# Pacing bulk loads, four tap buffers and grouped TensorE switches in a planned convolution and feed-forward kernel

## Chip, cores and metric

The kernel runs on one core of one Trainium2 chip. The metric is the device time of one execution in microseconds (us). A measurement of this kernel is the median of several executions.

## What is computed

The reference mixes a state-space convolution and a feed-forward layer by a gate that depends on the token. Cut to what matters (2048 tokens, 640 channels, 128 states, 1728 hidden columns, all float32):

```python
g = sigmoid((u * gate_w).sum(-1, keepdims=True))           # one gate per token
K = 2 * einsum("dn,dnl->dl", C, exp(A*dt * arange(2048))).real  # 2048 filter taps for each of 640 channels
y = irfft(rfft(u.T, 4096) * rfft(K, 4096))[:, :2048].T     # causal convolution along the tokens
a = y + u * D_skip
b = relu(u @ w1) @ w2                                      # 640 -> 1728 -> 640
out = g * a + (1 - g) * b
```

## The kernel before

**The feed-forward part.** Each float32 matrix is split into a high and a low half, and a product is three TensorE matmuls (high x high, high x low, low x high). The 1728 hidden columns are worked in three passes (`PARTS`, five, five and four slices of 128). A pass goes over 8 groups of 256 tokens. In the first pass `trans` turns the tokens (tile `xx`) and stores the halves in DRAM (`xt`), `hidden` makes hidden values from them, and `sums` multiplies by w2 and stores partial sums (`part`). In passes two and three `wide` makes hidden values for a pair of groups (matmuls of 512 columns, written W below), `sums` makes four sums a group (matmuls of 320 columns, S below), and `reload` brings the halves of the next pair back from `xt`: 1280 KB a group, two DMAs, both issued by one planned task.

**The convolution part.** First the taps are generated: phases, exponentials, sines and short matmuls (tiles `sn`, `cs`, `mg`, `G`, `pk`) give the taps, which go to DRAM as `kd`. Generation runs beside the first two passes. Then `conv` transforms in five groups of 128 channels, beside the rest of the feed-forward work. For a group: `load_k` brings four parts of the taps (`ck`, two buffers), `load_u` the tokens (`xu`, one buffer, 1 MB in two DMAs); `stage1` is four tasks for taps (K) and four for tokens (U), each of 8 recorded matmuls into a PSUM buffer `pc`, emptied by two VectorE transposes into the tile `ku`, which holds the K half and the U half of a group. `stage2` is eight tasks of 32 recorded matmuls; ScalarE copies one result into K's block, VectorE makes two products, one of them into `kx` (three buffers, `KX`), and GpSimd adds. `inv2` is two steps of 128 short matmuls; `relay` is eight VectorE transposes from U back into K; `inv1` is four tasks of two matmuls (Y below), whose results ScalarE scales by the gate into `yo` (two buffers, `YO`). From `yo` they go to the output, after GpSimd has added the feed-forward sum (`yj`), or to DRAM (`y_`), to be added in the last pass. PSUM has three `pc` buffers, shared by all these steps.

**What sets the order.** Every step is a task of the class `Plan` with an engine, a queue, a cost set by hand, its dependencies, and the buffers (rings) that it takes and uses. `Plan.run` goes through planned time: for each engine it takes the head of a queue with the lowest priority number among those that are ready, and adds half a rank to a task whose mode differs from the engine's current one (`f` for the feed-forward and for phases and exponentials, `t` for taps, `c` and `c1` for the convolution). For TensorE it also looks `HOLD` = 0.3 ahead: a task of better priority that is nearly ready is waited for. It has a cost for loading TensorE's code, once in 128 matmuls, greater when a bulk transfer is under way. A chosen task's instructions are emitted at once, and `Pinned` (line 287 in the profile, for all of them) keeps them in that order. So the order on every engine, and on SyncE (SP), which issues nearly all DMAs one after another, is fixed when the program is built. An instruction that has to wait holds up all that stand behind it on its engine.

Of the kernel before, what the change touches and what calls it, by code (L numbers as in the profile page):

```python
# [31 lines left out]
KX = 3  # L32
# [22 lines left out]
S2D = 1  # L55
# [6 lines left out]
YO = 2  # L62
YJ = 2
# [79 lines left out]
class Plan:  # L143
# [7 lines left out]
    SLACK = .8  # L151

# [53 lines left out]

    def run(self):
        self.free = {e: 0.0 for e in self.LAG}
        mode, dma, log, done, block = {}, 0.0, [], 50.0, 0.0
        heads = {k: 0 for k in self.queues}  # L210
        while True:
            best = None
            for e in self.LAG:
                c, soon = [], []
                for (eng, q), n in heads.items():
                    if eng == e and n < len(self.queues[eng, q]):
                        t = self.queues[eng, q][n]
                        r, known = self.ready(t)
                        for g in t.glue:
                            r2, k2 = self.ready(g)  # L220
                            r, known = max(r, r2), known and k2
                            for b in t.take:
                                k = sum(x.ring is b.ring for x in (*t.take, *g.take))
                                r = max(r, sorted(b.ring.slots)[k - 1] if len(b.ring.slots) >= k else 1e9)
                        (c if known else soon).append((r, t))
                if not c:
                    continue
                at = max(self.free[e], min(r for r, _ in c))
                key = lambda t: t.prio + (0.5 if t.mode is not None and mode.get(e) not in (None, t.mode) else 0)
                r, t = min((x for x in c if x[0] <= at), key=lambda x: key(x[1]))  # L230
                start = max(at, r)
                if e == 'PE':

                    for r2, t2 in c:
                        if key(t2) < key(t) and r2 <= at + self.HOLD:
                            t, start = t2, max(at, r2)
                    hold = [r2 for r2, t2 in soon if t2.prio < t.prio and r2 <= at + self.HOLD]
                    if hold:
                        at = max(hold)
                if best is None or at < best[0]:  # L240
                    best = at, e, t, start
            if best is None:
                break
            _, e, t, start = best
            change = self.CHANGE.get(e, 0) if t.mode is not None and mode.get(e) not in (None, t.mode) else 0
            if t.mode is not None:
                mode[e] = t.mode
            for b in t.take:
                b.ring.slots.remove(min(b.ring.slots))
            t.fn()  # L250
            self.free[e] = start + change + t.dur
            if e == 'PE':

                done += t.n
                while done >= 128:
                    done -= 128
                    at = self.free[e] - t.dur * done / t.n
                    fetch = self.FETCH + (self.BUSY if dma > at + 2 else 0)
                    self.free[e] += max(0, block + fetch - at)
                    block = max(at, block + fetch)  # L260
            if t.port:

                self.free[e] += 0.25 * min(max(self.free['POOL'] - start, 0), t.dur)
            t.end = self.free[e] + t.lag
            if t.kb:
                dma = max(dma, start + min(t.dur, 0.62) + 0.5) + t.kb / (230 if start < 12 else 270)
                t.end = max(dma, start + t.dur) + 1.1
            for b in (*t.take, *t.use):
                b.left -= 1
                b.free = max(b.free, t.end)  # L270
                if b.left == 0:
                    b.ring.slots.append(b.free)
            heads[e, t.q] += 1
            log.append((start, t))
# [6 lines left out]
class Pinned:  # L281
# [3 lines left out]
    def __getattr__(self, name):  # L285
        f = getattr(self._eng, name)
        return lambda *a, **k: self._tc.keep_in_program_order(f(*a, **k))  # L287
# [21 lines left out]
class Kernel:  # L309
    def __init__(self, tc, ctx, io, out):  # L310
# [4 lines left out]
        self.plan, self.late_loads = Plan(), []  # L315
# [23 lines left out]
    def feed_forward(self):  # L339
# [151 lines left out]
        def reload(p, g):  # L491
            x_ = xtok[p, g] = tok('xhl')

            def load():
                for l in range(2):
                    D_.dma_start(self.xx[:, l, g % 2].bitcast(F32), sc['xt'][g][l])
            X[p, g] = [A('SP', 'x', 1.25, load, [xst[g], xst[7]], take=[x_], kb=1280, rank=2)]

        W, H, done, stq = {}, {}, {}, S if STQ == 'ACT' else D_
# [111 lines left out]
        def sums(p, g, j, q_, qld):  # L611
# [16 lines left out]
            def pe(ks):  # L628
                def go():
                    if ks[0] == 0:  # L630
                        st['sb', g, j] = pb.tile([128, 320], F32, name="pf")
                    for k in ks:
# [3 lines left out]
                                      start=k == 0, stop=k == np_ - 1)  # L636
                return go
# [14 lines left out]
            for k in range(0, np_, 4 if j == 0 else 5):  # L652
# [4 lines left out]
                           use=[w for _, w in ws] + list(ht) + ([b_] if k else []), mode='f'))  # L657
            e = A('ACT' if p == 0 else 'DVE', 'ff', 0.38 if p == 0 else 0.43, out, a + qld, take=[q_] if p == 0 and j == 0 else (),
# [88 lines left out]
        for p, n in enumerate(PARTS):  # L747
# [3 lines left out]
            for k, g in enumerate(order):  # L751
# [28 lines left out]
                if not last:  # L780
# [5 lines left out]
                    continue  # L786
                to, ds = CG[g] * 128, []
                for t in range(2):
# [16 lines left out]
                    es = [sums(p, g, j, q_, mx[t]) for j in (2 * t, 2 * t + 1)]  # L805
                    if CG[g] == 5 and g <= FIRST:
                        es.append(with_last(g, t, q_, es))
# [355 lines left out]
    def conv(self, C=128):  # L1163
# [5 lines left out]
        for k, v in dict(psc=3, ck=2, cu=1, kx=KX, yo=2, yj=2, K=2).items():  # L1169
            ring(k, v)  # L1170
# [16 lines left out]
        def load_k(i, q):  # L1187
            k_ = tok('ck')

            def go():  # L1190
                t = st['ck', i, q] = self.early.tile([128, 16, 32], F32, name="ck", bufs=2)
# [6 lines left out]
        def load_u(i):  # L1198
            u_ = tok('cu')

            def go():
                if i == 0:
                    self.xu = self.early.tile([128, 4 * D], F32, name="xu")
                t = st['cu', i] = self.xu[:, :16 * C].rearrange("p (b d) -> p b d", d=C)
                for h in range(2):
                    D_.dma_start(t[64 * h:64 * h + 64], ud[:, 16 * h:16 * h + 16, i * C:i * C + C])
            return u_, A('SP', 'cu', 1.6, go, [], take=[u_], kb=1200, rank=2.5 if i else 6)
# [9 lines left out]
        def paired(x, order):  # L1217
            return x.rearrange(f"p (j e m t) -> {order}", j=8, m=4, t=2)


        def stage1(kind, i, q, src):
# [15 lines left out]
            def turn(h):  # L1237
                def go():
                    if k and q == 0 and h == 0:
                        st['ku', i] = self.pr.tile([128, 2, 32 * C], F32, name="ku", bufs=2)  # L1240
                        st['K', i], st['U', i] = st['ku', i][:, 0], st['ku', i][:, 1]
# [9 lines left out]
            a = A('PE', 's' + kind, 0.87, pe, [ld, tf, opened] + ([] if k else [first[i]]), take=[b_, buf] if new else [b_], use=[s_] if new else [s_, buf],  # L1251
# [12 lines left out]
        def stage2(i, j, dep):  # L1264
            b_, x_ = tok('psc'), tok('kx')

            def pe():
                ps = self.psc.tile([128, 2, 4, C], F32, name="pc")
                for a in range(2):
                    for m in range(4):  # L1270
                        for p in range(2):
                            r, g = slice(p * 64, p * 64 + 64), 4 * j + m
                            x = st['ku', i].rearrange("p k (j e m t) -> p j m k e t", j=8, m=4, t=2)
                            self.E.matmul(ps[32 * m:32 * m + 32, p, 2 * a:2 * a + 2].rearrange("q k (e t) -> q k e t", t=2),
                                          st['tm'][r, g, 32 * a:32 * a + 32], x[r, j, m], start=True, stop=True)
                st['p2', i, j] = ps.rearrange("q p (a k) c -> q k a p c", a=2)

# [3 lines left out]
            def mul(a):  # L1281
                def go():
                    k = whole(i, j)
                    if a:
                        st['kx', i, j] = self.pr.tile([128, 2, 2, C], F32, name="kx", bufs=KX)
                    V.tensor_mul(st['kx', i, j] if a else k, st['p2', i, j][:, 1, None, a].to_broadcast([128, 2, 2, C]), k)
                return go

            def add(k):
                def go():  # L1290
                    y, x = whole(i, j)[:, k], st['kx', i, j][:, 1 - k]
# [4 lines left out]
            for a in (1, 0):  # L1296
                c.append(A('DVE', 's2', 0.62, mul(a), c, take=[x_] if a else (), use=[b_, K[i]] + [x_] * (1 - a), rank=S2D))
            return f, [A('POOL', 's2', 0.7, add(k), c, use=[x_, K[i]], rank=1) for k in range(2)]


        def whole(i, j):
            return st['K', i][:, 512 * j:512 * j + 512].rearrange("q (b p c) -> q b p c", b=2, p=2)


        def inv2(i, h, dep):
# [14 lines left out]
            def back(k):  # L1320
                def go():
                    S.copy(st['U', i].rearrange("q (h g m c) -> q h m g c", h=2, m=4, c=C)[:, h, 2 * k:2 * k + 2],
# [11 lines left out]
        def relay(i, r, dep):  # L1334
            d = slice(r * 16, r * 16 + 16)
            return A('DVE', 'rl', 0.95, lambda: V.transpose(out=st['K', i].rearrange("p (j d m) -> p d j m", j=8, m=4)[:, d],
                                                            in_=st['U', i].rearrange("p (j m d) -> p d j m", j=8, m=4)[:, d]),
# [5 lines left out]
        def inv1(i, j, dep):  # L1343
            last = i == n - 1
            for q in range(2):
# [8 lines left out]
                def pe(q=q, b0=b0):  # L1354
                    py = st['p4', i, b0] = self.psc.tile([128, 2, 4, C], F32, name="pc")
                    for h in range(2):
                        x = (h * 16 + b0) * C
                        self.E.matmul(py[h * 64:h * 64 + 64, 0].rearrange("p b c -> p (b c)"), st['tw'],
                                      st['K', i][:, x:x + 4 * C], start=True, stop=True)

                def copy(q=q, b0=b0, ns=ns, y_=y_, first=first):
                    if first:
                        self.gy = self.pr.tile([128, 2, 32 * C], F32, name="ku", bufs=2)[:, 0].rearrange("p (b c) -> p b c", c=C)
# [55 lines left out]
        self.u_first = u[1]  # L1419
# [4 lines left out]
        for i in range(n):  # L1424
            more = i + 1 < n
            if more:
                u = load_u(i + 1)
            fs = [stage2(i, j, [*dep, tm]) for j in range(8)]
# [61 lines left out]
```

## Time and profile before

| What | Value |
|---|---|
| Median of 3 runs | 666.48 us (666.0 to 666.77) |
| The profiled execution's own time | 668.51 us |
| Its span, first to last instruction | 666.7 us |
| VectorE busy | 524.2 us (79%), 818 instructions |
| ScalarE busy | 402.0 us (60%), 603 instructions |
| GpSimd busy | 93.7 us (14%), 133 instructions |
| Main DMA queue | 76058 packets, 101.16 MB, 50.8% of 16 engines |

The page gives the busy time of every engine, the span in 40 slices, and the chain of work that ended last. The first 60% of the span is the feed-forward passes one and two beside the generation of taps; from about 410 us on, the convolution runs beside pass three. "Issue" is a wait that no recorded event explains. A busy TensorE counts from the first matmul's start to the modelled end of the last, so short pauses between matmuls do not all show as idle.

### The profile page before, as it was taken

The page shows a single profiled execution, that of the slowest core. Times are in us where ns is not written, and L with a number is a line of the kernel's source. Part 1 is how long each engine was busy: PE and PEld are TensorE (multiplying, and loading weights), DVE is VectorE, ACT ScalarE, POOL GpSimd, SP SyncE. Part 2 cuts the span into 40 slices and gives each one's busy share as a digit, 9 for nine tenths or more (in the row PEclk, how much of TensorE's full clock was granted, in tenths as well). Part 3 has the DMA queues.
Part 4 walks back from the last instruction along what each step waited for, and adds up shares of the span by engine and source line. Part 5 has one row for each costly group of instructions (what it writes and reads, how often), then busy time and mean ns, then how long its engine had stood idle before and what let it go on. Part 6 is the DMA issues. An engine that isn't in the chain of part 4 may idle for free.

```text
span 666.7 us, 19238 instructions
## 1 busy us (share of the span) xinstructions
PE 630.3 (95%) x8236; PEld 505.5 (76%) x8236; DVE 524.2 (79%) x818; ACT 402.0 (60%) x603; POOL 93.7 (14%) x133
## 2 busy tenths in 40 slices
PE   7989999999999999999999999998999897978997
PEld 7989999899887887888998986845666444733666
DVE  5799838989999998989999985584995375977462
ACT  5467449998999989889789922042430541353431
POOL 0000000000000000000000000060600260623632
PEclk9999999999999999999999999999999997989999
DMA  9965744323364642441543149954068639245256
GB/s 264 315 214 184 238 143 159 113 73 135 105 198 123 235 121 65 174 151 57 199 144 96 57 146 286 293 169 97 3 218 177 191 96 249 62 120 132 59 167 137
DMA packets 76303, 102.80 MB, mean 154 GB/s; under 512 B 7609, under 2 KB 59449, under 8 KB 75962
## 3 DMA queue, kind: packets, MB, share of 16 engines
q1 hardware_dynamic: 76058, 101.16, 50.8%
q8 instruction: 65, 1.06, 0.7%
q10 hardware_dynamic: 160, 0.41, 0.2%
q14 instruction: 20, 0.16, 0.1%
HBM read 62.36 MB, written 39.19 MB: 152 GB/s over the span
## 4 chain that ended last, share of the span: by engine, by line
PE 60%; DVE 17%; DMA 9%; issue 4%; SPq 4%; ACT 3%; POOL 1%; DVEq 0%; ACTq 0%; POOLq 0%
PE pf L287 37%; PE pc L287 12%; PE pk L287 5%; SPq L287 4%; DMA xu<-in_A_u_dram 3%; DVE G L287 3%; DVE sn L287 3%; PE pg L287 2%; PE px L287 2%; DVE ku L287 2%; DMA ck<-kd 2%; DVE mg L287 2%; DVE cs L287 1%; DVE kx L287 1%; PE pe L287 1%
## 5 line engine op out<-in xcount | busy, mean ns | idle before, releaser
L287 PE MATMUL pf<-xx,w1h 128*128 128x256 f32 (+1 forms) x760 | 184.8, 340 | 2.1 <-issue 1.4
L287 PEld LDWEIGHTS pf<-xx,w1h 128*128 128x128 f32 x760 | 124.8, 189 | 27.9 <-issue 13.1
L287 PE MATMUL pf<-xx,w1l 128*128 128x512 f32 (+1 forms) x340 | 115.7, 340 | 0.0
L287 ACT COPY ku<-pc 128x512 f32<-128x512 f32 (+1 forms) x60 | 42.8, 731 | 91.7 <-PE pc L287 91.4
L287 PE MATMUL pf<-w2h,hh 128*128 128x320 f32 x288 | 90.4, 318 | 2.4 <-DVE hl L287 1.3
L287 PE MATMUL pf<-w2l,hh 128*128 128x320 f32 x288 | 88.0, 310 | 0.0
L287 PE MATMUL pf<-w2h,hl 128*128 128x320 f32 x256 | 74.1, 315 | 0.3 <-issue 0.3
L287 DVE STREAM_TRANSPOSE ku<-pc 128x512 f32<-128x512 f32 x80 | 50.8, 687 | 24.8 <-PE pc L287 24.7
L287 PEld LDWEIGHTS pf<-xx,w1l 128*128 128x128 f32 x340 | 64.3, 189 | 7.7 <-DVE w1l L287 0.2
L287 POOL TENSOR_TENSOR ku<-ku,kx 128x256 f32<-128x256 f32 x80 | 56.5, 739 | 96.2 <-DVE ku L287 38.6
L287 POOL TENSOR_TENSOR kt<-kt,dsk 128x8 f32<-128x8 f32 x20 | 10.1, 504 | 389.5 <-DVE kt L287 363.4
L287 PEld LDWEIGHTS pf<-w2h,hh 128*128 128x128 f32 x288 | 54.3, 189 | 10.8 <-issue 6.1
L287 PEld LDWEIGHTS pf<-w2l,hh 128*128 128x128 f32 x288 | 54.4, 189 | 0.5
L287 ACT ACT_TABLE_LOAD x42 | 53.9, 1283 | 0.7
L287 DVE TENSOR_TENSOR sn<-pg,cs 128x1024 f32<-128x1024 f32 x40 | 48.6, 1215 | 5.9 <-ACT cs L287 5.7
L287 DVE STREAM_TRANSPOSE ku<-ku 128x512 f32<-128x512 f32 x40 | 40.7, 1077 | 15.5 <-ACT ku L287 15.4
L287 ACT CAST cs<-pg 128x1024 int32<-128x1024 f32 x40 | 40.4, 1010 | 20.6 <-PE pg L287 20.5
L287 PEld LDWEIGHTS pf<-w2h,hl 128*128 128x128 f32 x256 | 46.7, 189 | 6.7 <-issue 6.3
L287 DVE TENSOR_TENSOR mg<-mg,cs 128x1024 f32<-128x1024 f32 x40 | 48.9, 1222 | 1.6
L287 ACT ACTIVATE cs<-cs,half_pi 128x1024 f32<-128x1024 f32 x40 | 45.6, 1141 | 0.0
L287 PE MATMUL pc<-ku,tm 64*32 64x256 f32 x1280 | 43.2, 397 | 0.5 <-DVE ku L287 0.5
L287 ACT ACTIVATE sn<-sn 128x1024 f32<-128x1024 f32 x40 | 42.2, 1055 | 0.2
(169 smaller groups left out, 1249.1 us busy)
## 6 DMA issues: line engine op xcount, KB each, us to landing
xx<-xt SPq DMA_DIRECT2D x24, 640.0 KB, 6.8
xt<-xx SPq DMA_DIRECT2D x16, 640.0 KB, 3.7
part<-q SPq DMA_DIRECT2D x16, 640.0 KB, 3.5
q<-part SPq DMA_DIRECT2D x16, 640.0 KB, 4.6
ws<-in_B_w_dram SPq DMA_DIRECT2D x20, 320.0 KB, 4.8
kd<-kt SPq DMA_DIRECT2D x80, 64.0 KB, 1.9
ck<-kd SPq DMA_DIRECT2D x40, 128.0 KB, 4.1
xu<-in_A_u_dram SPq DMA_DIRECT2D x10, 512.0 KB, 11.4
```

Source lines behind the costliest of these rows:

```text
L287: return lambda *a, **k: self._tc.keep_in_program_order(f(*a, **k))
```

## The change

Six edits that go together:

1. **Planner.** While TensorE is in mode `f`, a convolution task is taken only if `burst` finds at least `GATHER` = 2 tasks of modes `c` or `c1` that could run in a row, or if `PATIENCE` = 3 have passed since the last task that was not `f`; otherwise the best ready `f` task is taken. The 0.3 look-ahead no longer applies between two `f` tasks.
2. **Reload of xx.** One task of two DMAs becomes two tasks of one DMA (640 KB). In pass three, three of the four tasks of a pair wait for the last matmul of a named sum (`last_of`, `mark`, `behind`); the wait stands on SyncE.
3. **Load of xu.** For groups 2 to 4 (counted from 0) the two DMAs become eight (128 KB each), two behind each of the first four `stage2` tasks of the group before.
4. **Taps.** Parts 1 and 3 of groups 1 to 4 (counted from 0) have two buffers of their own (`cl`), so there are four.
5. **Products over U's block.** `ku` is laid out so that the K and U parts of a block of 512 lie next to each other; the product that went to `kx` goes over U's part of the block, and `kx` is gone.
6. **Buffers of yo.** Three in place of two. The planned cost of a relay step goes from 0.95 to 1.02.

```diff
-KX = 3
...
-YO = 2
+YO = 3
...
+    BURST, GATHER, PATIENCE = ('c', 'c1'), 2, 3
...
+    def burst(self, c, heads, at):
+        run, end, taken = 0, at, {}
+        for _, t in sorted((x for x in c if x[1].mode in self.BURST), key=lambda x: x[0]):
+            for x in self.queues['PE', t.q][heads['PE', t.q]:][:self.GATHER]:
+                if x.mode not in self.BURST or any(d.end is None or d.end > end + .1 for d in x.deps):
+                    break
+                fits = True
+                for b in x.take:
+                    k = taken[b.ring] = taken.get(b.ring, 0) + 1
+                    fits = fits and k <= len(b.ring.slots) and sorted(b.ring.slots)[k - 1] <= end + .1
+                if not fits:
+                    break
+                run, end = run + 1, end + x.dur
+        return run
...
-                if e == 'PE':
+                if e == 'PE' and mode.get(e) == 'f':
+
+
+                    if t.mode in self.BURST and at - since < self.PATIENCE and self.burst(c, heads, at) < self.GATHER:
+                        other = [x for x in c if x[1].mode == 'f' and x[0] <= at + .05]
+                        if other:
+                            r, t = min(other, key=lambda x: key(x[1]))
+                            start = max(at, r)
+                if e == 'PE' and (t.mode != 'f' or mode.get(e) != 'f'):
...
+            if e == 'PE' and t.mode != 'f':
+                since = start + t.dur
...
+    def behind(self, ins, mark):
+        info = mybir.DependencyInfo(mybir.DependencyClass.Sync, mybir.DependencyReason.DATA)
+        self._tc.add_manual_dep(ins.ins, mark, info, reason="paced")
...
-            def load():
-                for l in range(2):
-                    D_.dma_start(self.xx[:, l, g % 2].bitcast(F32), sc['xt'][g][l])
-            X[p, g] = [A('SP', 'x', 1.25, load, [xst[g], xst[7]], take=[x_], kb=1280, rank=2)]
-
+            def load(l):
+                x = D_.dma_start(self.xx[:, l, g % 2].bitcast(F32), sc['xt'][g][l])
+                for t in X[p, g][l].deps:
+                    if t in self.mark:
+                        D_.behind(x, self.mark[t])
+            X[p, g] = [A('SP', 'x', 0.62, lambda l=l: load(l), [xst[g], xst[7]], take=() if l else [x_], use=[x_] if l else (),
+                         kb=640, rank=2) for l in range(2)]
...
+                if k % 2 == 0 and k < 6:
+                    paced = [x for i in order[k + 2:k + 4] for x in X[p, i]]
...
+                    for x in (paced[1:3], paced[3:])[t] if k % 2 == 0 and k < 6 else ():
+                        x.deps += (last_of[p, g, 2 * t + (x is not paced[1])],)
...
-            k_ = tok('ck')
+            own = q % 2 and i
+            k_ = tok('ckp' if own else 'ck')
...
-            def go():
-                if i == 0:
-                    self.xu = self.early.tile([128, 4 * D], F32, name="xu")
-                t = st['cu', i] = self.xu[:, :16 * C].rearrange("p (b d) -> p b d", d=C)
+            def go(k):
+                if k == 0:
+                    if i == 0:
+                        self.xu = self.early.tile([128, 4 * D], F32, name="xu")
+                    st['cu', i] = self.xu[:, :16 * C].rearrange("p (b d) -> p b d", d=C)
+                t, b = st['cu', i], slice(k * 16 // n, (k + 1) * 16 // n)
                 for h in range(2):
-                    D_.dma_start(t[64 * h:64 * h + 64], ud[:, 16 * h:16 * h + 16, i * C:i * C + C])
-            return u_, A('SP', 'cu', 1.6, go, [], take=[u_], kb=1200, rank=2.5 if i else 6)
+                    x = D_.dma_start(t[64 * h:64 * h + 64, b], ud[:, 16 * h:16 * h + 16, i * C:i * C + C][:, b])
+                    if behind:
+                        D_.behind(x, self.mark[behind[k]])
...
-                        st['ku', i] = self.pr.tile([128, 2, 32 * C], F32, name="ku", bufs=2)
-                        st['K', i], st['U', i] = st['ku', i][:, 0], st['ku', i][:, 1]
+                        st['ku', i] = self.pr.tile([128, 8, 2, 512], F32, name="ku", bufs=2)
+                        st['K', i], st['U', i] = st['ku', i][:, :, 0], st['ku', i][:, :, 1]
...
-                    if a:
-                        st['kx', i, j] = self.pr.tile([128, 2, 2, C], F32, name="kx", bufs=KX)
-                    V.tensor_mul(st['kx', i, j] if a else k, st['p2', i, j][:, 1, None, a].to_broadcast([128, 2, 2, C]), k)
+                    V.tensor_mul(whole(i, j, 'U') if a else k, st['p2', i, j][:, 1, None, a].to_broadcast([128, 2, 2, C]), k)
...
-                u = load_u(i + 1)
-            fs = [stage2(i, j, [*dep, tm]) for j in range(8)]
+                u = load_u(i + 1, [f for f, _ in fs[:4]] if i else ())
```

## Prediction made before the run

> **What bounds the kernel now.** I read the page first, then busy time by stretches, then TensorE's and SyncE's timelines where TensorE stands still, then the waits. The page:
>
> ```profile
> span 666.7 us, 19238 instructions
> PE 630.3 (95%) x8236; PEld 505.5 (76%) x8236; DVE 524.2 (79%) x818; ACT 402.0 (60%) x603; POOL 93.7 (14%) x133
> PE 60%; DVE 17%; DMA 9%; issue 4%; SPq 4%; ACT 3%; POOL 1%; DVEq 0%; ACTq 0%; POOLq 0%
> ```
>
> TensorE is busy 95% of the span and leads the chain, so there are 666.7 - 630.3 = 36.4 us of idle time to win, plus what its busy time hides. By stretches (busy time of each engine, then granted clock, DMA share and GB/s):
>
> ```profile
> 100.00:400.00 300.00, 293.67 (x3995) 261.08 (x3994) 282.34 (x418) 263.29 (x314) 9.87 (x19) 1.00 0.40 130
> 410.00:662.00 252.00, 234.21 (x3525) 147.10 (x3524) 165.88 (x245) 80.84 (x165) 82.73 (x106) 0.97 0.55 152
> 458.00:470.00 12.00, 10.05 (x278) 6.40 (x264) 3.19 (x5) 5.53 (x7) 0.23 (x1) 0.86 0.25 57
> 516.00:524.00 8.00, 5.62 (x29) 3.05 (x27) 0.93 (x2) 4.10 (x11) 0.97 (x1) 1.00 0.68 215
> 553.00:567.00 14.00, 9.99 (x180) 6.97 (x182) 6.11 (x10) 1.98 (x3) 0.00 (x0) 0.76 1.10 298
> 590.00:601.00 11.00, 6.89 (x40) 2.54 (x43) 8.86 (x12) 3.79 (x11) 2.43 (x3) 0.84 0.51 129
> ```
>
> In generation (100 to 400 us) TensorE is idle for only 300 - 293.67 = 6.3 us, with VectorE at 94%: little to win. In the convolution (410 to 662 us) it is idle for 252 - 234.21 = 17.8 us, and no other engine passes 66%. So the change is worth what it does to TensorE's stops there. The last four rows hold most of them. TensorE's timeline around each (start, length, operation, and in brackets the idle time and what ended it):
>
> ```profile
> 460.13 1.40 PE L287 MATMUL pc<-ku,tn 32*64 32x128 f32 x76
> 463.48 1.97 PE L287 MATMUL pc<-ku,tn 32*64 32x128 f32 x52 [1.95 <-issue]
> 521.91 1.09 PE L287 MATMUL pc<-ck,tf 64*64 64x512 f32 x8 [2.38 <-ACT yo L287]
> 555.33 1.62 PE L287 MATMUL pc<-ku,tn 32*64 32x128 f32 x92
> 560.96 1.54 PE L287 MATMUL pc<-ku,tn 32*64 32x128 f32 x36 [4.01 <-issue]
> 592.99 0.31 PE L287 MATMUL pf<-w2h,w2l 128*128 128x320 f32 x1
> 597.20 1.99 PE L287 MATMUL pc<-ck,tf 64*64 64x512 f32 x8 [3.90 <-issue]
> ```
>
> The stops at 461.5 and 556.9 us come inside an `inv2` step, after 76 and 92 of 128 matmuls, where no buffer changes hands: no semaphore explains them. I take them for late loads of TensorE's code. The stop at 519.5 us is a wait for ScalarE's `yo`; that at 593.3 us stands ahead of a taps step. SyncE's timeline shows what was under way:
>
> ```profile
> 451.59 1.35 SPq L287 DMA_DIRECT2D xu<-in_A_u_dram  x2
> 453.13 4.38 SPq L287 DMA_DIRECT2D ck<-kd  x4
> 550.72 1.34 SPq L287 DMA_DIRECT2D xu<-in_A_u_dram  x2
> 552.11 3.25 SPq L287 DMA_DIRECT2D ck<-kd  x4
> 555.40 4.08 SPq L287 DMA_DIRECT2D xx<-xt  x4
> 592.44 1.26 SPq L287 DMA_DIRECT2D ck<-kd  x2
> ```
>
> Before 556.9 us some 4 MB were issued within 9 us (1 MB xu, 0.5 MB ck, 2.5 MB xx), before 461.5 us 1.5 MB. At 592.44 us taps are issued only when the taps steps before them had freed their two buffers; the TensorE step that wants them starts at 597.20 us. With the landing times (KB each, median us from issue to landing)
>
> ```profile
> xx<-xt SPq DMA_DIRECT2D x12, 640.0 KB, 6.8
> xu<-in_A_u_dram SPq DMA_DIRECT2D x10, 512.0 KB, 11.4
> ck<-kd SPq DMA_DIRECT2D x36, 128.0 KB, 4.3
> q8 instruction: 29, 0.48, 0.8%
> ```
>
> 592.44 + 4.3 = 596.7 us, about when TensorE goes on: this stop is the taps' buffer. The last row, of the DMA queues from 400 us on, says that code arrives by DMA, 29 packets of 16 KB, among everything else.
>
> **What each stop costs.** Idle time, plus the slow clock that follows (12 us at 0.86 lose 0.14 x 12):
> - 461.5 us: 1.95 + 0.14 x 12 = 3.6 us
> - 519.5 us: 2.4 us, the clock stays at 1.00
> - 556.9 us: 4.01 + 0.24 x 14 = 7.4 us
> - 593.3 us: 3.90 + 0.16 x 11 = 5.7 us
>
> Together 19.1 us. [...]
>
> **The change, part by part.**
>
> *Switches.* In the two programs as built, TensorE goes between feed-forward and convolution 96 times from the first convolution step on before, 74 times after: 11 round trips fewer. The price of one, from steps of 32 matmuls:
>
> ```profile
> 432.48 0.31 PE L287 MATMUL pf<-w2h,w1l 128*128 128x320 f32 x1
> 432.63 0.31 PE L287 MATMUL pf<-w2h,w2h 128*128 128x320 f32 x1
> 432.87 2.98 PE L287 MATMUL pc<-ku,tm 64*32 64x256 f32 x96
> 435.78 0.41 PE L287 MATMUL pf<-w2l,w2h 128*128 128x320 f32 x1
> 436.03 0.31 PE L287 MATMUL pf<-w2h,w2l 128*128 128x320 f32 x1
> 436.35 1.15 PE L287 MATMUL pc<-ku,tm 64*32 64x256 f32 x32
> 437.44 0.73 PE L287 MATMUL pf<-xx,w1h 128*128 128x512 f32 x2
> ```
>
> Three steps in a row take 435.78 - 432.87 = 2.91 us, one alone 437.44 - 436.35 = 1.09 us; so a step is (2.91 - 1.09) / 2 = 0.91 us and leaving the convolution costs 0.18 us. Entering it takes 436.35 - 436.03 = 0.32 us where two such matmuls follow each other at 0.15 us: 0.17 us. Round trip 0.35 us, 11 of them **-3.9 us**.
>
> *yo in three buffers, taps in four.* They take away what the second and fourth stops waited for, 2.4 + 5.7 = **-8.1 us**. ScalarE's own waits tell how often stores of `yo` were late:
>
> ```profile
> ACT yo L287 <- DMA out_dram<-yo: 17.6, 5, 7.9
> ```
>
> Next late after the taps would be their transposes, on a VectorE that is free a third of the time here.
>
> *Pacing.* xx comes in DMAs of 640 KB behind sums, xu in eighths behind `stage2` steps, so less stands ahead of a code load. Bounds: nothing of the first and third stops goes (0), or all of it (3.6 + 7.4 = 11.0 us). I take two thirds, nearer to the upper row, as both stops follow such a burst: **-7.3 us**. The 18 more DMAs for xu cost SyncE about 0.65 us each (1.34 us for two, above), 12 us spread over three groups, off TensorE's path while SyncE is ahead. What is queued behind a waiting xu or xx load: taps, `yj`, `q`, and the stores of `yo` that ScalarE waits for.
>
> *Products over U's block.* The same instructions on other addresses, so 0 by themselves; no wait for `kx` to come free is left. VectorE is as busy as before.
>
> ```profile
> L287 DVE TENSOR_TENSOR kx<-pc,ku x40: 643/680/699, 434.8 to 623.7; 128x512 f32<-128x512 f32 x40
> L287 DVE TENSOR_TENSOR ku<-pc,ku x40: 678/691/693, 435.5 to 624.8; 128x512 f32<-128x512 f32 x40
> L287 DVE STREAM_TRANSPOSE ku<-ku x40: 994/1080/1164, 467.2 to 643.3; 128x512 f32<-128x512 f32 x40
> 644.42 3.65 PE L287 MATMUL pc<-ku,tw 128*64 128x512 f32 x16 [0.98 <-DVE ku L287]
> ```
>
> *Given back.* A `stage2` step costs TensorE 0.91 us and VectorE 0.68 + 0.69 = 1.37 us, with three `pc` buffers: a run of four or more steps waits 0.46 us for each step past the third. The runs are of two or three, with four to eight steps close together in places; I take 2 us (bounds 0, and 0.46 x 40 = 18 if every step waited). Longer runs of short matmuls also use up code faster: one new stop like the first, 3.6 us. Last, ahead of the last Y steps stand 42 W and 8 S in place of 48 W and 4 S, by 0.23 and 0.147 us each 0.8 us less cover for eight transposes of 1.08 us, and TensorE waited 0.98 us there already: 0.8 us. **+6.4 us** in all.
>
> *The look-ahead between f tasks* reorders generation a little: the number of matmuls before the first convolution step is the same in both programs. At most the 6.3 us of idle time above goes, or as much is added; I take 0.
>
> Sum: -3.9 - 8.1 - 7.3 + 6.4 = **-12.9 us**. On the profiled execution's span that is 666.7 - 12.9 = 653.8 us, on its own time (668.51 us) 655.6 us. That execution lies 2.0 us above the median of the runs, so the median after should be 666.5 - 12.9 = **653.6 us**.
>
> **The rivals.**
>
> 1. *The code stops stay.* Had code loads been late because short matmuls outrun them, pacing would win nothing and longer runs would lose. For it: both stops are in `inv2`, the densest step, and the first has a DMA share of only 0.25 in its stretch. Against it: the longer stop has 1.10. Time: -3.9 - 8.1 + 6.4 = -5.6, so 660.9 us.
> 2. *All stops go and nothing comes back*: -3.9 - 19.1 + 0.8 = -22.2, so 644.3 us. Against it: three `pc` buffers and VectorE's 1.37 us a step remain.
> 3. *Slower: SyncE held by its own waits.* A load that waits for a TensorE mark holds the stores of `yo` behind it; ScalarE then waits for a `yo` buffer and keeps a `pc` buffer, and TensorE stops as at 519.5 us or 593.3 us. It decides once a store is held longer than it takes to fill three `yo` buffers. For it: 24 of the xu DMAs and 9 of the xx DMAs now wait. Against it: the marks are placed before the stores in planned order. At 5.7 us twice in each of the three paced groups it costs 34 us if nothing overlaps; I price one in each group plus the 2.4 us kind once: 19.5 us, giving -12.9 + 19.5 = +6.6, so 673.1 us.
> 4. *The change doesn't do what it says.* The switches did fall from 96 to 74 in the built order, so this is left only for pacing, which is rival 1.
>
> **How the numbers follow.** Forecast (-17 to -8 us) 0.42; rival 1 (-8 to -1.4) 0.25; rival 2 (below -17) 0.13; no change 0.05; rival 3 0.15. A measurement of this kernel tells about 0.2% (1.3 us) from no change. Faster 0.80, same 0.05, slower 0.15. The range reaches to rival 2 and to the edge of no change, 644 to 667 us.
>
> **What would show it.** Right: no idle time of TensorE over 2 us at a taps step or behind `yo`; stops inside `inv2` shorter than 2 us, and a granted clock of 1.00 in most stretches after 410 us; the same busy time of VectorE and GpSimd. Wrong: ScalarE's `yo` waiting for stores as long as before (17.6 us) or longer, which is rival 3; a stop of 2 us or more inside `inv2` or `stage2` with few bulk bytes under way, which is rival 1; VectorE ending most of TensorE's waits in `stage2`, which would make 2 us too small; or generation ending more than 3 us later than before, which my 0 for the look-ahead leaves out.

## The result, and the profile after

The changed kernel took 650.66 us (median of 4, 649.17 to 651.5) against 666.49 us: a ratio of 0.976 with a 95% interval of 0.973 to 0.980. In a second session it took 650.30 us against 667.31 us, 0.973 (0.969 to 0.976). That is 16 to 17 us less, and about 3 us below the forecast of 653.6 us. It lies inside the forecast's range, but this range also takes in the first two rivals, so that alone is a weak test. The profiled execution took 649.88 us, 18.6 us less than the profiled one before; by the medians it is 15.8 us. Its page, then busy time by stretches (PE, PEld, DVE, ACT, POOL, then granted clock, DMA share, GB/s):

```profile
span 648.1 us, 19256 instructions
PE 620.6 (96%) x8236; PEld 505.5 (78%) x8236; DVE 523.1 (81%) x818; ACT 401.4 (62%) x603; POOL 93.8 (14%) x133
```

```profile
100.00:400.00 300.00, 293.54 (x3881) 262.98 (x3881) 280.96 (x416) 263.95 (x315) 10.10 (x19) 0.99 0.40 133
408.00:648.00 240.00, 226.51 (x3525) 146.57 (x3524) 164.88 (x245) 80.62 (x165) 82.64 (x106) 0.98 0.56 162
458.00:470.00 12.00, 11.78 (x243) 6.89 (x243) 11.27 (x17) 5.63 (x10) 8.46 (x12) 1.00 0.32 90
513.00:521.00 8.00, 6.13 (x71) 3.57 (x72) 4.15 (x6) 4.19 (x9) 4.30 (x6) 0.57 0.79 221
553.00:567.00 14.00, 14.00 (x306) 11.35 (x291) 13.86 (x20) 5.47 (x8) 9.05 (x13) 1.00 0.48 154
575.00:595.00 20.00, 16.61 (x184) 6.86 (x186) 16.30 (x25) 7.07 (x20) 5.39 (x6) 1.00 0.66 199
```

TensorE's idle time over the span fell from 36.4 to 27.5 us, and its busy time from 630.3 to 620.6 us for the same 8236 matmuls: about half of the 18.6 us of span is stops that went, half is busy time, which fits fewer switches and less slow clock (by the clock records a granted share of 0.50 for 13.65 us up to TensorE's last matmul before, for 10.24 us after, 3.41 of these in generation). Generation is as it was (6.5 us idle in place of 6.3). In the convolution, counted from its first matmul to TensorE's last one, the idle time fell from 17.5 to 8.0 us. (The second row leaves 13.5 us idle, but 5.4 us of that come after TensorE's last matmul, which ends at 642.6 us. Before, it ended at 661.8 us, so only 0.2 of the prediction's 17.8 us were of this kind.) TensorE's timeline shows three stops of over 1 us there, and a step of `inv2`, in which two of the old stops stood, now always runs through (the first, middle and last of ten):

```profile
439.86 2.11 PE L314 MATMUL pc<-ku,tn 32*64 32x128 f32 x128
...
514.87 1.53 PE L314 MATMUL pc<-ku,tm 64*32 64x256 f32 x24 [3.13 <-ACT yo L314]
523.41 2.10 PE L314 MATMUL pc<-ku,tn 32*64 32x128 f32 x128
...
581.19 3.91 PE L314 MATMUL pc<-xu,tf 64*64 64x512 f32 x32 [1.48 <-issue]
592.42 0.92 PE L314 MATMUL pc<-ku,tm 64*32 64x256 f32 x24 [1.38 <-DVE ku L314]
612.14 2.09 PE L314 MATMUL pc<-ku,tn 32*64 32x128 f32 x128
```

So both stops inside `inv2` are gone. In place of the one of 3.90 us ahead of a taps step there is one of 1.48 us ahead of a tokens step. The one behind ScalarE is still there and larger: 3.13 us, and after it the clock was 0.57 for 8 us, another 3.4 us. That breaks one of the prediction's signs of being right, no idle time over 2 us behind `yo`. A second profile of the changed kernel (experiment 12) has the three stops again, at 3.74, 1.50 and 1.43 us, one more of 1.46 us, and none inside `inv2`.

### The profile page after: what moved, and what is told of

Same layout as the page of the kernel before. It is cut to its first block, busy times and chain, and to the rows that moved or that the text cites. A ratio compares the mean times of both kernels' runs of the same rounds, so it can differ in the third digit from the quotient of the medians.

```text
span 648.1 us, 19256 instructions
## 1 busy us (share of the span) xinstructions
PE 620.6 (96%) x8236; PEld 505.5 (78%) x8236; DVE 523.1 (81%) x818; ACT 401.4 (62%) x603; POOL 93.8 (14%) x133
## 4 chain that ended last, share of the span: by engine, by line
PE 67%; DVE 15%; DMA 7%; ACT 4%; SPq 4%; issue 2%; POOL 0%; ACTq 0%; DVEq 0%; POOLq 0%
PE pf L314 44%; PE pc L314 11%; PE pk L314 6%; DVE ku L314 5%; SPq L314 4%; PE pg L314 3%; PE px L314 2%; DMA q<-part 2%; DMA part<-q 2%; DVE sn L314 2%; DVE G L314 1%; DMA xu<-in_A_u_dram 1%; DVE mg L314 1%; PE pe L314 1%; ACT ku L314 1%
## 5 line engine op out<-in xcount | busy, mean ns | idle before, releaser
L314 DVE TENSOR_TENSOR ku<-pc,ku 128x512 f32<-128x512 f32 x80 | 52.7, 685 | 17.5 <-ACT ku L314 16.3
L314 POOL TENSOR_TENSOR ku<-ku 128x256 f32<-128x256 f32 x80 | 56.4, 739 | 63.3 <-DVE ku L314 43.3
L314 ACT ACTIVATE hh<-pf 128x512 fp32r<-128x512 f32 (+1 forms) x40 | 20.6, 514 | 43.9 <-PE pf L314 43.9
```

The lines of the kernel that those rows point to most:

```text
L314: self._last = self._tc.keep_in_program_order(f(*a, **k))
```

## The experiments

Two theories stood against each other. The prediction's: the terms are separate (switches, buffers of `yo` and of the taps, bulk loads in the way of code), each with its price. The rival: the new order is what does it, and single parts are worth nothing or harm.

**1. The planner alone, on the kernel before.** All of the diff's lines in `Plan`, nothing else.

> The kernel before with the planner's edit alone (no pacing, old buffers, old layout). TensorE now switches 72 times between feed-forward and convolution in place of 96. Terms are independent (the prediction's theory): 24 x 0.175 us = 4.2 us less, the four stops of 2.4 to 7.4 us stay, 2 us come back in longer runs: 662 to 665 us. Rival, the planner's order is what removed the stops: 656 us or less, with no idle time of TensorE over 2 us at a taps step or behind yo.

Measured: 671.47 us against 666.8, ratio 1.008 (1.005 to 1.010): slower, outside what either theory expected. Switches fell to 72, but the idle time in the convolution grew from 17.5 to 20.4 us, and the stretch after TensorE's last matmul from 5.0 to 7.9 us. TensorE's timeline at the longest stops:

```profile
504.89 5.40 PE L314 MATMUL pc<-xu,tf 64*64 64x512 f32 x32 [4.74 <-issue]
...
563.33 1.55 PE L314 MATMUL pc<-ku,tn 32*64 32x128 f32 x38 [3.53 <-issue]
...
599.37 1.13 PE L314 MATMUL pc<-ck,tf 64*64 64x512 f32 x4 [5.43 <-issue]
```

One of them is inside `inv2`. The other two stand ahead of a tokens and of a taps step, where the kernel before has one of 3.90 us; experiments 7 to 10 go into that place. With two `yo` buffers and bulk loads as before, convolution steps in a row seem to run into the same shortages harder; no run shows that link by itself. What is shown is that the terms are not separate.

**2. Everything but the planner**, and later **3. only the look-ahead kept.**

```diff
-                if e == 'PE' and mode.get(e) == 'f':
...
-                if e == 'PE' and (t.mode != 'f' or mode.get(e) != 'f'):
+                if e == 'PE':
```

(For the second of the two only the last pair of lines.)

> The changed kernel with the old planner: 116 switches in place of 74. Independent terms: 42 x 0.175 = 7.4 us more than the changed kernel's 650.7, so 656 to 659 us. Rival, buffers and pacing need the new planner to be worth anything: 664 us or more. Rival, the planner wins nothing and its longer runs cost what fewer switches save: 650 to 652 us.

> The changed kernel with the old look-ahead of 0.3 also between two feed-forward tasks; the rule of two convolution tasks in a row stays. If the look-ahead matters little (the prediction's 0): within 2 us of the changed kernel's 650.7, and the first convolution step starts within 2 us of 408. If leaving it away was worth part of the gain: 653 us or more, with more switches or a later first convolution step.

Measured: 664.1 us, ratio 0.995 (0.993 to 0.997), and 663.65 us, 0.995 (0.992 to 0.998). Both have 116 switches, and the two programs as built have the same instructions in the same order on every engine. With the look-ahead kept the rule of two in a row does nothing: it picks a feed-forward task, and the loop behind it finds the convolution task, ready and of better rank, and takes it back. Beside these buffers and this pacing the planner is worth some 13 us (663.65 us, or 663.24 without the two longest of its twelve runs, against 650.30 us in one session). The busy time in the convolution shows it, for the kernel with the look-ahead kept:

```profile
405.00:661.00 256.00, 238.44 (x3542) 150.40 (x3540) 167.16 (x246) 82.57 (x168) 82.71 (x106) 0.99 0.55 155
```

3.0 of these busy us come before 408 us. From 408 us to its last matmul TensorE is busy for 235.4 us in place of the 226.5 after the change, for as many matmuls (3522 and 3525), and idle for 11.8 in place of 8.0 us. So of the 13 us some 9 are busy time and 4 are idle time. By the prediction's price, 21 round trips at 0.35 us explain 7.4 of the 9; that is an estimate, no run shows it.

**4. No pacing.** `reload` and `load_u` as before, with the new buffers, layout and planner:

```diff
-                u = load_u(i + 1, [f for f, _ in fs[:4]] if i else ())
+                u = load_u(i + 1)
...
-                    for x in (paced[1:3], paced[3:])[t] if k % 2 == 0 and k < 6 else ():
-                        x.deps += (last_of[p, g, 2 * t + (x is not paced[1])],)
```

> The changed kernel, xx and xu loaded as before (one task of two DMAs each, no waits on TensorE marks), 72 switches. If bulk loads delay TensorE's code: stops inside inv2 or stage2 that end on issue come back, 5 to 9 us more, 656 to 660 us. If late code is a matter of dense matmuls alone: within 2 us of the changed kernel, 649 to 653 us.

Measured: 654.47 us, ratio 0.982 (0.978 to 0.986), 0.6 to 1.0% above the changed kernel's two ratios, so 4 to 6 us. Stops inside `inv2` are back, the longest right behind 2.5 MB of xx. TensorE's and SyncE's timelines:

```profile
564.63 1.42 PE L314 MATMUL pc<-ku,tn 32*64 32x128 f32 x78
568.96 1.03 PE L314 MATMUL pc<-ku,tn 32*64 32x128 f32 x50 [2.91 <-issue]
```

```profile
560.76 1.97 SPq L314 DMA_DIRECT2D xx<-xt  x4
```

**5. The kernel before without the bulk loads**, in its old order.

```diff
-                for h in range(2):
+                for h in range(0 if i > 1 else 2):
...
-                for l in range(2):
+                for l in range(0 if p > 1 else 2):
```

> The kernel before, in the same order, that leaves out the reload of xx in pass three and the load of xu for groups 2 to 4 (it computes on with what the buffers hold), so about 10.5 MB of bulk loads are missing. If bulk loads make the code late: the stops of 1.95 and 4.01 us inside inv2 and the slow clock after them go, the waits for taps and yo shrink; 11 us less, 653 to 657 us. If dense short matmuls do it: both stops inside inv2 stay, 662 to 667 us.

Measured: 655.75 us against 668.01, ratio 0.982 (0.979 to 0.986): 12 us less. The first stop in `inv2` is gone, the second is 1.00 us in place of 4.01. TensorE's timeline, and the stretch of the first stop:

```profile
458.82 2.10 PE L287 MATMUL pc<-ku,tn 32*64 32x128 f32 x128
...
550.60 0.87 PE L287 MATMUL pc<-ku,tn 32*64 32x128 f32 x35 [1.00 <-issue]
...
584.99 1.19 PE L287 MATMUL pc<-ck,tf 64*64 64x512 f32 x8 [3.84 <-issue]
```

```profile
458.00:470.00 12.00, 11.83 (x333) 6.91 (x331) 7.60 (x12) 7.05 (x11) 4.40 (x7) 1.00 0.01 3
```

Bulk loads made the stops inside `inv2`, with the same matmuls at the same density; 1 us is left without them. The stop at the taps (3.84 us) does not come from bulk loads. The stop behind `yo` at 519 us is gone too, so not all of the 12 us comes from the stops inside `inv2`.

That these stops are late code is a reading of the DMA records; no view says what a packet holds. The page of the kernel before lists the queue q8 as `instruction` (packets, MB, share of 16 engines):

```profile
q8 instruction: 65, 1.06, 0.7%
```

That is 65 packets of 16 KB in a run of 8236 matmuls, one for every 127 on average. One of them lands inside each of these stops or less than 1 us ahead of it, and TensorE goes on 1.3 to 1.7 us later: in the kernel before one lands at 462.05 us and TensorE goes on at 463.48, one at 559.28 and TensorE at 560.96; in experiment 4 at 567.64 and 568.96; here at 549.06 and 550.60. In the long stops ahead of taps and tokens steps none lands.

**6. The same order, without the waits of pacing** (`behind` does nothing).

> The changed kernel with the same order on every engine, the xx and xu loads no longer waiting for TensorE marks: SyncE issues each as soon as it gets to it and the buffer is free. If the waits themselves space the loads: stops inside inv2 or stage2 come back, 653 to 658 us. If the place of the smaller loads in SyncE's order is enough: 649 to 652 us. If the waits hold up stores and q loads (the stop of 3.13 us behind yo at 511 us): that stop shrinks, 646 to 649 us.

Measured: 650.18 us, ratio 0.973 (0.971 to 0.976): no difference. What helps in pacing is that the loads are smaller and where they stand in SyncE's order (the two were not tried apart), not that they wait for TensorE.

**7. The old buffers, 8. two tap buffers, 9. two yo buffers**, each on the changed kernel (`own = False` for the taps, `YO = 2`, or both).

> The changed kernel with two yo buffers and two tap buffers in all, 84 switches. If the buffers took away the stops at a taps step and behind yo: 8.1 us for them and 10 x 0.175 = 1.8 us for the switches, 658 to 662 us, with TensorE idle over 2 us at such places. Rival, these stops came from the order and not from the number of buffers: 650 to 653 us.

> The changed kernel with two tap buffers in place of four, 72 switches. If the taps' buffers took away the stop at 593 us: 3 to 6 us more, 653.5 to 657 us. If the planner or the third yo buffer did: 649.5 to 652 us.

> The changed kernel with two yo buffers in place of three, 76 switches. By the prediction's term 2.4 us more and 0.35 us for two switches: 652.5 to 655 us. If yo is held by late stores whatever the number of buffers (ScalarE waits 14.5 us for stores after the change, 17.6 before): 649.5 to 652 us.

Measured: both 658.57 us, ratio 0.988 (0.985 to 0.991); two tap buffers 647.88 us, 0.971 (0.968 to 0.973); two `yo` buffers 661.02 us, 0.990 (0.987 to 0.993). The third `yo` buffer is worth 1.4 to 1.7%, 9 to 11 us; the two more tap buffers nothing. In the profile with two `yo` buffers TensorE is idle for 6.0 us more in the convolution and busy for 4.6 us more than after the change, and the stretch after its last matmul is 2.8 us longer. With both old no stop of over 1 us stands ahead of a taps step: the longest are one of 3.50 us behind `yo` at 631 us and one of 2.55 us at 637 us. With four tap buffers and two of `yo` the stop ahead of a taps step is there, at 4.79 us. TensorE's, ScalarE's and VectorE's timelines:

```profile
590.20 1.98 PE L314 MATMUL pc<-cl,tf 64*64 64x512 f32 x8 [4.79 <-issue]
```

```profile
587.39 1.14 ACT L314 ACTIVATE yo<-pc,gate 128x128 f32<-128x128 f32 x4 [1.14 <-DMA out_dram<-yo]
590.32 1.14 ACT L314 ACTIVATE yo<-pc,gate 128x128 f32<-128x128 f32 x4 [1.79 <-DMA out_dram<-yo]
```

```profile
581.12 7.78 DVE L314 STREAM_TRANSPOSE ku<-ku 128x512 f32<-128x512 f32 x8 [3.19 <-ACT ku L314]
588.80 1.30 DVE L314 STREAM_TRANSPOSE ku<-pc 128x512 f32<-128x512 f32 x2
```

ScalarE waits for a store before it may write `yo`, so two Y steps keep two of the three `pc` buffers. The third holds the result of the taps step before, and the next taps step waits for it. VectorE empties it, but only after its eight relay transposes: it is done at 590.10 us, and TensorE goes on at 590.20. The hold by the Y steps formed a new theory for the stop at 593 us before. That stop ends in the same way, and its taps had come long before; VectorE's and SyncE's timelines of the kernel before:

```profile
588.09 7.81 DVE L287 STREAM_TRANSPOSE ku<-ku 128x512 f32<-128x512 f32 x8 [2.25 <-ACT ku L287]
595.81 1.29 DVE L287 STREAM_TRANSPOSE ku<-pc 128x512 f32<-128x512 f32 x2
```

```profile
564.48 1.09 SPq L287 DMA_DIRECT2D ck<-kd  x2
```

VectorE was done at 597.10 us, and TensorE went on at 597.20; the semaphore that TensorE's sequencer stood at was VectorE's. The taps of this step are those issued at 564.48 us, and the later of the two loads had landed at 570.4 us (the step waits for the semaphores of these two loads). The pair issued at 592.44 us is for a later step.

**10. A third yo buffer in the kernel before, same order.** The planner goes on with two; the product goes over U's block, in the old layout, to make room.

```diff
-YO = 2
+YO = 3
...
-                        st['kx', i, j] = self.pr.tile([128, 2, 2, C], F32, name="kx", bufs=KX)
+                        st['kx', i, j] = whole(i, j, 'U')
```

> The kernel before in exactly its order on every engine, with a third yo buffer in the pool that the planner does not know of (the product for kx goes over U's block to make room). If the stop of 3.90 us ahead of a taps step at 593 us was PSUM held by Y steps whose yo was not yet stored (new theory, after the kernel with four tap buffers and two yo buffers kept a stop of 4.79 us there): both that stop and the one of 2.38 us at 519 us go, 656 to 660 us at a median before of 667. If it was the landing of the taps (the prediction's reading): only the one at 519 us goes, 663 to 666 us.

Measured: 690.28 us against 667.31, ratio 1.034 (1.031 to 1.036): slower, as neither theory expected. Its timelines give three answers. ScalarE's, for the place that was at 593 us, and TensorE's:

```profile
609.72 1.20 ACT L287 ACTIVATE yo<-pc,gate 128x128 f32<-128x128 f32 x4
613.86 1.14 ACT L287 ACTIVATE yo<-pc,gate 128x128 f32<-128x128 f32 x4 [2.94 <-DMA out_dram<-yo]
```

```profile
476.34 3.58 PE L287 MATMUL pc<-ku,tm 64*32 64x256 f32 x64 [0.92 <-DVE ku L287]
482.19 1.15 PE L287 MATMUL pc<-ku,tm 64*32 64x256 f32 x32 [1.38 <-DVE ku L287]
...
611.62 1.09 PE L287 MATMUL pc<-ck,tf 64*64 64x512 f32 x8
615.62 3.14 PE L287 MATMUL pc<-xu,tf 64*64 64x512 f32 x16 [2.90 <-issue]
```

The third copy into `yo` no longer waits (2.89 us before), and the taps step follows the one before it after 2.2 us in place of 6.2. The stop moves one step on, to a tokens step, and ends there as the old one did: TensorE goes on at 615.62 us, 0.1 us after VectorE has emptied the `pc` of the first taps step, behind the eight relay transposes. So the theory holds for the taps step, which now gets a `pc` that a Y step has left, but the stop had a second cause, on VectorE. The stop that was at 519 us stays, at 2.3 in place of 2.4 us, so no lack of `yo` buffers made it. And `stage2` steps now wait for VectorE. TensorE's waits for ScalarE and VectorE at these places (us in total, times, longest), the second 3.3 us in the kernel before:

```profile
PE pc L287 <- ACT yo L287: 2.3, 1, 2.3
PE pc L287 <- DVE ku L287: 18.9, 22, 1.4
```

The long waits among these end on a product (`ku<-pc,ku`). A `stage2` matmul reads the K and the U part of its block in one access, and in the old layout these lie 16 KB apart in a partition, with parts of other blocks between. That the built program therefore orders the product of one step against the matmuls of the next is a reading of the code, not tried by itself. In the new layout, with both parts side by side, the waits of this kind are 2.6 us in all. So the layout, priced at 0, seems to be what makes the third `yo` buffer affordable: the product over U's block frees `kx`'s 6 KB in each partition. The kernel before with the new layout and three `yo` buffers was not run.

**11. Two tap buffers and four of yo, 12. the changed kernel once more.**

> The changed kernel with two tap buffers and four yo buffers. If yo's buffers still hold TensorE up (stops behind ScalarE of 1.1 and 1.5 us remain with two tap and three yo buffers): 643 to 647 us. If three are enough: 647 to 650 us, as with two tap buffers alone.

> The changed kernel itself once more, beside the others on one chip. 649 to 652 us if its ratio to the kernel before holds at 0.976; the kernel with two tap buffers had 0.971, so a ratio of 0.973 or less here would mean that four tap buffers cost nothing.

Measured: 649.28 us, ratio 0.973 (0.970 to 0.976), and 650.30 us, 0.973 (0.969 to 0.976). Three `yo` buffers are enough. The kernels with two tap buffers may be 1 to 2 us ahead of the changed one, but the intervals overlap; no version clearly beats it.

## Why the prediction held, point by point

- **What bounds it, and where.** Right: up to the first convolution step TensorE is idle as long as before (13.9 us), so the gain lies in its stops and its busy time after 408 us; VectorE and GpSimd are as busy as before.
- **Switches, -3.9 us.** The count is right, but the count from 96 to 74 hid two changes: the new buffers with the old planner would have made it 116. Measured from there, beside the other edits, the planner is worth 13 us; alone, on the kernel before, it costs 5.
- **Buffers, -8.1 us.** Size about right (8 to 11 us), by luck, as both readings behind it were wrong. The stop at 593 us was not the landing of taps: it was a `pc` buffer that VectorE emptied late, and a `pc` was short because Y steps held two while `yo` waited for stores (experiments 7 to 10). The prediction named these transposes, but as what would be late next. The taps' buffers were worth nothing. And the stop at 519 us was no lack of `yo` buffers: ScalarE stood at `q`, and `yo` came behind it in its queue, after 19.93 us of idle time that ended on the load of `q`. ScalarE before, then after:

```profile
519.28 1.55 ACT L287 ACTIVATE q<-q,omg 128x640 f32<-128x640 f32 x2 [19.93 <-DMA q<-part]
520.74 2.16 ACT L287 ACTIVATE yo<-pc,gate 128x128 f32<-128x128 f32 x8
```

```profile
512.96 0.83 ACT L314 ACTIVATE q<-q,omg 128x640 f32<-128x640 f32 x1 [3.86 <-DMA xu<-in_A_u_dram]
513.70 1.12 ACT L314 ACTIVATE yo<-pc,gate 128x128 f32<-128x128 f32 x4
```

- **Rival 3 in small.** After the change SyncE shows what the load of `q` stands behind, four pieces of xu:

```profile
501.44 2.68 SPq L314 DMA_DIRECT2D yj<-part  x3
504.17 2.65 SPq L314 DMA_DIRECT2D xu<-in_A_u_dram  x4
506.86 0.60 SPq L314 DMA_DIRECT2D q<-part  x1
507.56 1.29 SPq L314 DMA_DIRECT2D out_dram<-yo  x2
```

  The term of -2.4 us became a cost: 3.13 us of idle time and 3.4 us of slow clock in place of 2.4. One such place was priced at 5.7 us in rival 3; there is one, not three, and ScalarE's waits for stores of `yo`, the sign named for this rival, fell from 17.6 to 14.5 us. Without the waits for marks a stop of 1.95 us is still there, and without any pacing (experiment 4) one of 1.39 us, so held loads and the 0.65 us for each issue can make up only a part of it.
- **Pacing, -7.3 us.** Bulk loads as the cause of the stops in `inv2` are right, by experiments 4 (one of 2.91 us is back) and 5 (1.00 us in place of 4.01); that TensorE's code is the link is a reading of the DMA records. Both stops in `inv2` are gone, 11.0 us by their rows, the upper bound; taken away by itself pacing costs 4 to 6 us. That it works by the waits was wrong: it works by size and place. The two thirds of 11.0 us were a guess between bounds, and the 4 to 6 us are somewhat less.
- **Given back, +6.4 us.** Mis-sized. No new code stop came (3.6 us priced); TensorE's waits for VectorE in `stage2` did not grow (2.6 us in all, below); ahead of the last Y steps it waited 0.57 us, not more than the 0.98 before. What came back instead was the stop above, and 1.48 and 1.38 us at 581 and 592 us. Both end on VectorE: it empties the `pc` of the first taps step at 581.10 us, again behind relay transposes, and TensorE goes on at 581.19.

```profile
PE pc L314 <- DVE ku L314: 2.6, 5, 1.4
```

- **Look-ahead, 0.** The step that failed as it was put: this is no reordering of generation but the other half of the switching rule, which has no effect without it (experiment 3). The forecast wasn't hurt because the switches had been counted in the built order, with both halves in.

So the sum came out 3 to 4 us short of the gain, with terms that were partly right for the wrong reason. What stays open: how much of the 9 us of busy time that the planner saves is switches, and what in detail makes up the 9 to 11 us of the third `yo` buffer.

## What to carry to other kernels

Count switches and stops in the built order and price each stop by its own row, but ask of every stop what the engine that released it had itself been waiting for: the stop at 519 us had its cause one engine further back, in ScalarE's queue, and the one at 593 us, marked as "issue", had one on VectorE and one in the stores that ScalarE waited for. Parts of a change that share buffers don't add up: the planner alone made this kernel 0.8% slower and, with a third output buffer and smaller loads, 2% faster. The large loads here needed no waits to be paced (0.973 of the kernel before without the waits, 0.973 to 0.976 with them); splitting them and placing them between others in the queue was enough, and each piece cost about 0.65 us of issue time in front of what stood behind it.

## What the runs showed of the hardware

- A stop of TensorE was followed by a slower clock after 1.95 us of idle time in the kernel before (0.86 over 12 us), but not after 2.38 us there (1.00 over 8 us); after the change 3.13 us brought 0.57 over 8 us. In the clock records of these three stretches the granted share is 0.50 for 3.41 us, not lowered at all, and 0.50 for 6.83 us. So here a stop's second cost came to as much as its first (3.4 us beside 3.13), and idle time alone did not tell whether it came.
- Bulk loads made TensorE stop where it waited for no buffer: the same 128 short matmuls took 2.10 us with a DMA share of 0.01 around them (experiment 5), and stopped for 1.95 us in the middle with 1.5 MB issued in the 10 us before (the kernel before). A packet of 16 KB on the queue listed as `instruction` had landed 1.43 us before TensorE went on. That this packet was TensorE's late code is a reading of these times.
